# A fused attention, Fourier mixing and MLP kernel on one core: the written order of its work is replaced behind the last loads of the second weight matrix

## The chip, the cores and the metric

The kernel runs on one core of one Trainium2 chip. The metric is the time of one execution in microseconds of device time; less is better. A core has a matrix engine (TensorE, PE in the profile), a vector engine (VectorE, DVE), a scalar engine (ScalarE, ACT), a general engine (GpSimd, POOL) and a queue that only issues transfers (SyncE, SP). Each runs its own list of instructions strictly in order. What one needs of another, it waits for by semaphore, and everything behind a waiting instruction on that engine waits too. The matrix engine writes to banks of PSUM; an evacuation (an instruction of VectorE or ScalarE that reads a bank and writes to SBUF) makes a bank free again.

## The reference

```python
def attention(q, k, v, n_global, n_local):        # 4 batches, 8 heads, 768 rows, 64 wide
    scores = q @ k^T / 8 + bias                   # bias: -slope(head) * distance
    scores = where(is_global | is_local, scores, -1e9)  # 8 global keys, 96 local keys back
    a = exp(scores - max); a = a / sum(a)
    return a @ v
def moe(x, w1, w2):                               # x: attention out as (4, 768, 512); w1 512x2048, w2 2048x512
    mixed = real(fft(fft(x, axis=1), axis=2))
    u = x + mixed
    un = (u - mean(u)) / sqrt(var(u) + 1e-6)      # over the 512 features
    return u + relu(un @ w1) @ w2                 # the second u is the sum, not its norm
```

## The kernel before

The four batches go through the same stages, and the stages of different batches overlap.

*Attention.* q and k are loaded (GpSimd's queue casts them to half precision), transposed, and multiplied to scores in PSUM; ScalarE takes the exponential (`er`, L763), VectorE multiplies it with a mask that holds the bias (`ex`, L778; the mask `mk` is made by ScalarE, L1657), and TensorE multiplies with v (`av`, L822). The first rows of v are copied into `vB` (L793, L795). VectorE divides by the sums (`x`, L832 and L834).

*Mixing.* The two Fourier transforms are matrix products with cosine tables on folded halves of x: VectorE makes the folds (`f1`, `f2`, `f3`, `z`, `w`), TensorE the products `y` (L1105) and `u` (L1192). The rows of x are needed in another arrangement to be added: x is written to DRAM (`xd`; ScalarE's queue, L874), and read back by SyncE (`xr`, L884) and by a gather on GpSimd's queue (`xg`, L887), which takes its indices from `back`, that SyncE loads (L1608). In batch 1 the write consists of two transfers of 384 KB.

*Chunks.* A batch has three pairs of row blocks, so there are 12 chunks c = 0 to 11. Chunk 3 is the first of batch 1, 6 the first of batch 2. For each chunk VectorE adds u = x + mixed (`u c`, L1232 for most, L1244 to L1251 for the middle one of a batch, c = 1, 4, 7, 10, which needs xg), the row is centred (`un`, two halves, L1269 on ScalarE or L1271 on VectorE), transposed (`unT`; by a transfer of SyncE's from chunk 3 on, L1292), squared on ScalarE (`ss`, L1278), and the reciprocal deviation is made by GpSimd (`rstd`, L1285 and L1286).

*MLP.* The first product of a chunk has eight units `ph(c,0)` to `ph(c,7)` of eight matmuls of 256 columns each (L1339); each fills one bank, and its evacuation with the relu is `h c j` on ScalarE (L1344) or VectorE (L1345). The second product of chunks 0 and 1 is plain (`pg(c,t,part)`, L1370, each part with a quarter of w2; its sum into u is `ob`, L1381). From chunk 2 on it is a scheme with seven half products in place of eight, in units `p1`, `p45`, `p6`, `p7` and `p32` (L1484), which needs sums of h (`s 1` to `s 4`, VectorE, L1448 to L1461) and sums of w2. Of the sums of w2 there are `w2a` (L1420) and two folds `w2t 0` and `w2t 1` (L1424 to L1426, three instructions each), which are made once, by VectorE; `p45(2)` is the first that needs both folds. The results are added to u by VectorE (`ra`, `rd`, `ob`, L1502) and stored.

*What sets the order.* Everything is recorded as named units with the engines that may do it, and then put on the engines in the order of a table, `Plan.ORDER`, which holds for each of PE, ACT, DVE, POOL and SP a list of names (A for attention units, M for mixing, H for `ph`, G for the second product, T for the rest; `H27.0` is the first other operation that H27 issues). A name under ACT rather than DVE puts the operation on ScalarE. `Plan.run` (L291) walks the lists and keeps a clock for each engine with estimated costs; those estimates serve to find a table and to decide in which order the lists are emitted, and they are no part of what runs on the chip. PSUM banks and buffers are taken in rings in the order of the lists, so a unit waits for the evacuation of an earlier one that had the same bank.

## Time and profile before

| | |
|---|---|
| three runs | 246.40 us median, 246.03 to 246.49 |
| the profiled execution | 245.87 us; span in the trace 244.1 us |
| TensorE | busy 232.0 us of 244.1 |
| VectorE | busy 193.4 us |
| ScalarE | busy 138.8 us |
| GpSimd | busy 114.8 us, transfers that it issues included |
| DMA | 32.85 MB, mean 135 GB/s |

The profile is one execution. The span is the time from the first to the last instruction in the trace; 1.77 us of the execution lie around it. Rows of the timeline read: start, duration, engine, line of the kernel, operation, result and source, number of instructions, and in brackets how long the engine had been idle before and what it then waited for. The ends of matmuls are modelled, so that a unit of eight matmuls of 256 columns is shown with 1.04 us though the next one begins after 0.87 us.

### The profile page before, as it was taken

The page shows a single profiled execution, that of the slowest core. Times are in us where ns is not written, and L with a number is a line of the kernel's source. Part 1 is how long each engine was busy: PE and PEld are TensorE (multiplying, and loading weights), DVE is VectorE, ACT ScalarE, POOL GpSimd, SP SyncE. Part 2 cuts the span into 40 slices and gives each one's busy share as a digit, 9 for nine tenths or more (in the row PEclk, how much of TensorE's full clock was granted, in tenths as well). Part 3 has the DMA queues.
Part 4 walks back from the last instruction along what each step waited for, and adds up shares of the span by engine and source line. Part 5 has one row for each costly group of instructions (what it writes and reads, how often), then busy time and mean ns, then how long its engine had stood idle before and what let it go on. Part 6 is the DMA issues. An engine that isn't in the chain of part 4 may idle for free.

```text
span 244.1 us, 7606 instructions
## 1 busy us (share of the span) xinstructions
PE 232.0 (95%) x3251; PEld 191.2 (78%) x3251; DVE 193.4 (79%) x420; ACT 138.8 (57%) x226; POOL 114.8 (47%) x164
## 2 busy tenths in 40 slices
PE   7679899999999999999999999999999999999993
PEld 2557776878677667788989888898889898888883
DVE  2559997879972789999999889889998755846483
ACT  2368788864657468658357788364534651434200
POOL 8998898866590038999059056500300320011020
PEclk9997999999999999999999999999999999999999
DMA  6999999999999999999999979220570330040212
GB/s 170 181 169 145 157 235 172 197 190 196 110 145 152 234 179 205 117 135 110 242 184 285 135 84 156 46 33 13 174 258 4 77 99 0 1 130 1 89 72 99
DMA packets 95938, 32.85 MB, mean 135 GB/s; under 512 B 84160, under 2 KB 92480, under 8 KB 95904
## 3 DMA queue, kind: packets, MB, share of 16 engines
q0 software_dynamic: 66176, 17.06, 71.7%
q1 hardware_dynamic: 26560, 12.56, 25.1%
q10 hardware_dynamic: 3168, 2.75, 4.1%
q8 instruction: 25, 0.41, 0.7%
q14 instruction: 9, 0.07, 0.1%
HBM read 31.44 MB, written 8.65 MB: 164 GB/s over the span
## 4 chain that ended last, share of the span: by engine, by line
PE 67%; DMA 14%; DVE 5%; ACT 5%; POOL 3%; issue 3%; SPq 1%; POOLq 0%
PE ph L1339 29%; PE pgD L1484 14%; PE pgA L1484 10%; DMA qk<-in_q_dram 4%; DMA v<-in_v_dram 4%; PE py L1105 3%; DMA hT<-in_q_dram 3%; PE pg L1370 3%; PE pav L822 3%; ACT ex L766 2%; DMA back<-backm 2%; DMA xr<-xd,back 2%; PE sc L737 2%; PE pu L1192 1%; ACT mk L1657 1%
## 5 line engine op out<-in xcount | busy, mean ns | idle before, releaser
L1339 PE MATMUL ph<-unT,w 128*128 128x256 f16 x768 | 94.4, 273 | 0.8 <-issue 0.4
L1339 PEld LDWEIGHTS <-w 128*128 128x128 f16 x768 | 73.6, 98 | 12.5 <-issue 1.2
L1344 ACT ACTIVATE hT<-ph 128x512 f16<-128x512 f32 x73 | 42.9, 596 | 54.6 <-PE ph L1339 52.6
L1484 PEld LDWEIGHTS <-hT 128*128 128x128 f16 x320 | 31.0, 98 | 4.3 <-issue 0.4
L1285 POOL TENSOR_SCALAR sm<-sm 128x2 f32<-128x2 f32 x12 | 3.4, 284 | 58.2 <-ACT un L1278 57.8
L763 ACT ACTIVATE er<-sc 128x1024 f16<-128x1024 f32 (+1 forms) x24 | 22.3, 951 | 11.4 <-PE sc L737 8.2
L1345 DVE TENSOR_SCALAR hT<-ph 128x512 f16<-128x512 f32 x23 | 15.7, 687 | 12.7 <-PE ph L1339 12.7
L766 ACT ACTIVATE ex<-sc 128x1024 f16<-128x1024 f32 (+1 forms) x24 | 21.7, 955 | 7.1 <-PE sc L743 6.9
L1502 DVE SCALAR_TENSOR_TENSOR u<-pgA,sm,u 128x256 f32<-128x256 f32 (+1 forms) x30 | 16.9, 568 | 6.4 <-PE pgA L1484 6.0
L1502 DVE SCALAR_TENSOR_TENSOR u<-pgD,sm,u 128x512 f32<-128x512 f32 (+1 forms) x21 | 15.2, 722 | 3.5 <-PE pgD L1484 3.3
L1355 POOL DMA_INDIRECT out_dram<-u,back x4 | 4.5, 1120 | 27.5 <-DVE rev L1140 16.3
L887 POOL DMA_INDIRECT xr<-xd,back x3 | 4.8, 1602 | 25.4 <-PE pg L1370 16.1
L1370 PE MATMUL pg<-w,hT 128*128 128x512 f16 x64 | 16.0, 379 | 0.0
L1118 ACT ACTIVATE zy<-py 128x1024 f16<-128x1024 f32 (+1 forms) x13 | 11.1, 857 | 8.4 <-PE py L1105 6.1
L778 DVE TENSOR_TENSOR ex<-er,mk 128x1024 f16<-128x1024 f16 (+1 forms) x24 | 15.1, 646 | 0.7 <-ACT er L763 0.7
L1278 ACT ACTIVATE un<-un 128x512 f16<-128x512 f16 x24 | 15.0, 625 | 1.1 <-DMA unT<-un 1.1
L552 POOL DMA_DIRECT2D qk<-in_k_dram x16 | 13.7, 903 | 1.2 <-DMA w<-in_moe_w_ch_dram 0.8
L1269 ACT ACTIVATE un<-u,sm 128x512 f16<-128x512 f32 x19 | 13.1, 717 | 1.9 <-DVE sm L1251 0.7
L552 POOL DMA_DIRECT2D qk<-in_q_dram x16 | 13.6, 870 | 0.0
L822 PEld LDWEIGHTS <-ex 128*128 128x128 f16 x352 | 12.4, 97 | 1.1 <-ACT ex L766 0.4
L834 DVE TENSOR_TENSOR x<-pav,rc 128x384 f16<-128x384 f32 x24 | 12.6, 554 | 0.6
L822 PE MATMUL pav<-v,ex 128*128 128x65 f16 x224 | 12.9, 193 | 0.2
(170 smaller groups left out, 492.9 us busy)
## 6 DMA issues: line engine op xcount, KB each, us to landing
w<-in_moe_w_ch_dram POOLq DMA_DIRECT2D x8, 512.0 KB, 13.4
out_dram<-u SPq DMA_DIRECT2D x15, 256.0 KB, 3.0
v<-in_v_dram POOLq DMA_DIRECT2D x12, 192.0 KB, 5.8
qk<-in_k_dram POOLq DMA_DIRECT2D x16, 96.0 KB, 5.4
qk<-in_q_dram POOLq DMA_DIRECT2D x16, 96.0 KB, 4.5
xr<-xd SPq DMA_DIRECT2D x3, 512.0 KB, 4.6
xd<-x ACTq DMA_DIRECT2D x2, 768.0 KB, 4.5
v<-in_v_dram POOLq DMA_DIRECT2D x8, 96.0 KB, 7.0
```

The costliest lines, as they stand in the source:

```text
L552: nc.gpsimd.dma_start(qk16[n][:, w, :, h], src[b, h0 + h].rearrange("(i m) d -> m i d", m=P))
L763: A(mine(), cut(pa), AF.Exp, 0.0, 0.125)
L766: A(cut(expst[hp][:, :, g * 512:g * 512 + (384 if g == 2 else 512)]), cut(pa), AF.Exp, 0.0, 0.125)
L778: VT(o, mine(), m, op=ALU.mult)
L822: nc.tensor.matmul(o[:, s * 65:(s + 1) * 65], lhsT, w, start=(a == 0), stop=(a == len(ops) - 1), skip_group_check=True)
L1278: A(x, x, AF.Square, accum_out=MV[c][:, a, 2:3])
L1339: nc.tensor.matmul(ph[:, a * CH:(a + 1) * CH].rearrange("p (x m) -> p x m", x=2), W1[0][:, d, jb * P:(jb + 1) * P], UNT[c][:, :, d, :], st ...
L1344: pl.later([("ACT", act(512), lambda: A(dst, ph, AF.Relu)), ("DVE", dve(512), lambda: V.tensor_scalar_max(dst, ph, 0.0))], [], e, [("h", c ...
L1345: ("DVE", dve(512), lambda: V.tensor_scalar_max(dst, ph, 0.0))],
L1370: nc.tensor.matmul(pg, HT[c][:, jb, t * P:(t + 1) * P], W2[0][:, jb, :], start=(jb == 0), stop=(jb == NJ - 1))
L1484: nc.tensor.matmul(o, lhs(j), rhs(j), start=(first and j == 0), stop=(j == NK - 1), skip_group_check=True)
L1502: V.scalar_tensor_tensor(o, x, r(t), acc, op0=ALU.mult, op1=ALU.add)
```

## The change

The table keeps its order in the first 57 us of the run: TensorE's list is the same up to `ph(1,4)`, and those of the other engines up to about there. Behind that all five lists are new. TensorE has the same 3251 matmuls in another sequence. Among other things:

- GpSimd issues all loads of q, k and v of batch 2 first; `rstd 1` stood in the midst of them and now stands behind.
- Operations change their engine: two copies of `vB` go from GpSimd to ScalarE, one more `vB` and the mirrored rows `r` of batches 1 and 2 (three copies each, L1139 to L1141) from GpSimd to VectorE, one `vB` from VectorE to GpSimd; 19 operations from VectorE to ScalarE (16 evacuations `h`, one small scaling in chunk 2, a half `un` of chunks 3 and 4), 16 from ScalarE to VectorE (13 `h`, one `y` evacuation of batch 1, a half `un` of chunks 3 and 11).
- The last instruction of six `u` evacuations, 128x2 elements, multiplies with a tile and a constant instead of a constant.
- The estimates in `Plan` are changed. A way to make the sums `s` on GpSimd is added and the table doesn't use it.

The diff, of which the table's new rows are left out but for two:

```diff
@@ class Plan @@
+    ALONE = 1.54
-    LAT = {"ACT": 0.14, "DVE": 0.12, "POOL": 0.08}
+    LAT = {"ACT": 0.18, "DVE": 0.12, "POOL": 0.08}
...
     ORDER = {
         "PE": (
...
-            "A39 A29 M3 M9 A32 M7 A33 A40 M8 M10 A31 M6 A27 M11 M13 A44 H2 H7 A43 H4 H3 M12 A42 H0 H1 A41 H12 G4 H13 H11 G0 H6 H5 M14 G1 G5 G6 H15 G7 H14 "
+            "A39 A29 M3 M9 A32 M7 A33 A40 M8 M10 A31 M6 A27 M11 M13 A44 H2 H7 A43 H4 H3 M12 A42 H0 H1 A41 H12 H6 G4 G0 H13 G5 G1 H5 M14 H10 G6 G2 G3 H8 "
...
+        def cp_act():
+            A(vB[hp], v16[b % 2][:, h, 1:NS - 1, :], AF.Copy)
+            for r in rows:
+                A(vB[hp][r], head(r), AF.Copy)
-        pl.later([("POOL", 0.6 + 0.6 * len(rows), lambda: cp(nc.gpsimd)), ("DVE", 0.3 + 0.3 * len(rows), lambda: cp(V))], after, 0.0, [("vB", b, hp)], rank=RA(b))
+        pl.later([("POOL", 0.6 + 0.6 * len(rows), lambda: cp(nc.gpsimd)), ("DVE", 0.3 + 0.3 * len(rows), lambda: cp(V)), ("ACT", act(528) * (1 + len(rows)), cp_act)], after, 0.0, [("vB", b, hp)], rank=RA(b))
...
-            V.tensor_scalar_mul(sm[:, :, 1], sm[:, :, 0], -SC / Dm)
+            V.scalar_tensor_tensor(sm[:, :, 1], sm[:, :, 0], 2 * SC / Dm, mhalf, op0=ALU.mult, op1=ALU.mult)
...
+        def slow(fn):
+            return [("POOL", pool2(NK * P), lambda: fn(nc.gpsimd))] if c > 2 else []
...
-        pl.later([("DVE", us, s1)], hs + sfree(0), 0.0, [("s", c, 1)], rank=1)
+        pl.later([("DVE", us, s1)] + slow(s1), hs + sfree(0), 0.0, [("s", c, 1)], rank=1)
```

The lists of a few places follow, as they stand on the engines; the number behind a tile's name tells tiles of one kind apart.

**First place: the way of batch 1's x.** GpSimd before, in the loads of q and k of batch 2 (`qk`); `sm_1` is the tile that `rstd 1` works on:

```order
L552 DMA qk_4_1504<-in_k_dram 128x6x64
L552 DMA qk_2_1488<-in_k_dram 128x6x64
L552 DMA qk_5_1124<-in_k_dram 128x6x64
L1285 TENSOR_SCALAR sm_1_1013<-sm_1_1013 128x2
L1286 TENSOR_TENSOR sm_1_1013<-sm_1_1013,mhalf_78 128x2
L552 DMA qk_2_1488<-in_k_dram 128x6x64
L552 DMA qk_4_1504<-in_k_dram 128x6x64
L552 DMA qk_3_1036<-in_k_dram 128x6x64
```

GpSimd after, from the same load on:

```order
L562 DMA qk_4_1504<-in_k_dram 128x6x64
L562 DMA qk_2_1488<-in_k_dram 128x6x64
L562 DMA qk_5_1124<-in_k_dram 128x6x64
L562 DMA qk_4_1504<-in_k_dram 128x6x64
L562 DMA qk_3_1036<-in_q_dram 128x6x64 x2
L562 DMA qk_4_1504<-in_q_dram 128x6x64 x2
L562 DMA qk_3_1036<-in_k_dram 128x6x64
L562 DMA qk_2_1488<-in_q_dram 128x6x64
L532 DMA v160_84<-in_v_dram 128x12x64
L562 DMA qk_2_1488<-in_k_dram 128x6x64
L1299 TENSOR_SCALAR sm_1_1013<-sm_1_1013 128x2
L1300 TENSOR_TENSOR sm_1_1013<-sm_1_1013,mhalf_78 128x2
```

The loads of q, k and v stand together, and `rstd 1` behind the last of them. ScalarE before, where it issues the two writes of x to `xd` (L874); `zy` is the evacuation of `y`, `mk` the mask, `hT` an evacuation `h`:

```order
L1344 ACTIVATE hT_3_1538<-ph_1_0_1744 128x512
L1657 ACTIVATE mk_76<-distk_74 128x640
L874 DMA xd_1_1780<-tt_1_1401 64x6x512
L1118 ACTIVATE zy_3_1753<-py_1_1_1782 128x1024
L874 DMA xd_1_1780<-tt_1_1401 64x6x512
L1657 ACTIVATE mk_76<-distk_74 128x640 x4
L1344 ACTIVATE hT_4_1792<-ph_2_4_1813 128x512
```

ScalarE after:

```order
L1292 ACTIVATE un_2_1530,sm_2_1250<-un_2_1530 128x512
L1292 ACTIVATE un_1_1332,sm_1_1013<-un_1_1332 128x512
L1674 ACTIVATE mk_76<-distk_74 128x640 x2
L1358 ACTIVATE hT_4_1752<-ph_2_1_1753 128x512
L888 DMA xd_1_1780<-tt_1_1411 64x6x512 x2
L1674 ACTIVATE mk_76<-distk_74 128x640 x3
L1292 ACTIVATE un_2_1530,sm_2_1250<-un_2_1530 128x512
L1674 ACTIVATE mk_76<-distk_74 128x640
```

The two writes are one behind the other, and the evacuation of `py_1_1` that stood between them is no longer there (VectorE has it).

**Second place: the second fold of w2.** VectorE before, from the end of `u 4` on; the three rows with `w2_0` and `tt` are `w2t 1`, `eg_91` is `s 1` of chunk 2:

```order
L1249 TENSOR_TENSOR sm_4_2075<-sm_4_2075 128x2
L1250 TENSOR_TENSOR sm_4_2075<-sm_4_2075,u_6_2074 128x2
L1251 TENSOR_SCALAR sm_4_2075<-sm_4_2075 128x2
L1424 TENSOR_TENSOR w2_0_711<-w2_0_711 128x4x256
L1425 TENSOR_TENSOR tt_2_1996<-w2_0_711 128x1024
L1426 TENSOR_TENSOR tt_2_1996<-w2_0_711,tt_2_1996 128x1024
L778 TENSOR_TENSOR ex2_82<-er_4_2030,mk_76 128x2x384
L1448 TENSOR_TENSOR eg_91<-hT_4_1792 128x1024
L778 TENSOR_TENSOR ex0_80<-er_5_2085,mk_76 128x2x512
```

VectorE after, from the end of `u 4` on:

```order
L1265 SCALAR_TENSOR_TENSOR sm_4_2068<-sm_4_2068,mhalf_78 128x2
L788 TENSOR_TENSOR ex0_80<-er_4_2020,mk_76 128x2x512
L1153 COPY rev0_1_2124<-zy_3_1733 128x2
L1154 COPY rev0_1_2124<-zy_3_1733 128x2x127
L1155 COPY rev0_1_2124<-zy_3_1733 128x256
L788 TENSOR_TENSOR ex2_82<-er_5_2065,mk_76 128x2x384
L1285 TENSOR_SCALAR un_4_2168<-u_6_2067,sm_4_2068 128x512
L1438 TENSOR_TENSOR w2_0_713<-w2_0_713 128x4x256
L1439 TENSOR_TENSOR tt_2_2008<-w2_0_713 128x1024
L1440 TENSOR_TENSOR tt_2_2008<-w2_0_713,tt_2_2008 128x1024
L1462 TENSOR_TENSOR eg_91<-hT_4_1752 128x1024
```

Two products `ex`, the three copies of mirrored rows (`rev0`) and a half `un 4` now stand ahead of the fold.

**Third place: the end.** VectorE before, from the last chunk's `s 1` on (`pgA_11`, `pgD_11` and `pgA_10`, `pgD_10` are banks of the last two chunks; L1448, L1454, L1461, L1451 are `s 1`, `s 2`, `s 4`, `s 3`):

```order
L1448 TENSOR_TENSOR mk_76<-hT_13_4340 128x1024
L1502 SCALAR_TENSOR_TENSOR u_12_3931<-pgA_10_4388,sm_10_3932,u_12_3931 128x256
L1454 TENSOR_TENSOR mk_76<-mk_76,hT_13_4340 128x1024
L1502 SCALAR_TENSOR_TENSOR u_12_3931<-pgD_10_4421,sm_10_3932,u_12_3931 128x512
L1502 SCALAR_TENSOR_TENSOR u_12_3931<-pgA_10_4388,sm_10_3932,u_12_3931 128x512
L1461 TENSOR_TENSOR mk_76<-hT_13_4340,mk_76 128x1024
L1451 TENSOR_TENSOR hT_13_4340<-hT_13_4340 128x8x128
L1502 SCALAR_TENSOR_TENSOR u_13_4090<-pgA_11_4497,sm_11_4091,u_13_4090 128x256
L1502 SCALAR_TENSOR_TENSOR u_13_4090<-pgD_11_4508,sm_11_4091,u_13_4090 128x512
L1502 SCALAR_TENSOR_TENSOR u_13_4090<-pgA_11_4497,sm_11_4091,u_13_4090 128x256
```

VectorE after:

```order
L1359 TENSOR_SCALAR hT_13_4339<-ph_11_4_4467 128x512
L1462 TENSOR_TENSOR mk_76<-hT_13_4339 128x1024
L1519 SCALAR_TENSOR_TENSOR u_12_3957<-pgD_10_4386,sm_10_3958,u_12_3957 128x512
L1468 TENSOR_TENSOR mk_76<-mk_76,hT_13_4339 128x1024
L1519 SCALAR_TENSOR_TENSOR u_13_4199<-pgA_11_4495,sm_11_4200,u_13_4199 128x256
L1475 TENSOR_TENSOR mk_76<-hT_13_4339,mk_76 128x1024
L1465 TENSOR_TENSOR hT_13_4339<-hT_13_4339 128x8x128
L1519 SCALAR_TENSOR_TENSOR u_13_4199<-pgD_11_4506,sm_11_4200,u_13_4199 128x512
L1519 SCALAR_TENSOR_TENSOR u_13_4199<-pgA_11_4495,sm_11_4200,u_13_4199 128x256
```

An evacuation of the last chunk stands directly ahead of its sums, one sum of chunk 10 (`pgA_10`) is ahead of them, and `s 4` and `s 3` stand behind the first `pgA_11`.

91 lines of the change are left out of this document (49 added, 42 removed), and 52 rows, old and new, of the table ORDER.

## The prediction

> **What bounds the kernel now.** I read first the busy times of the engines, then busy time by stretch, then what TensorE waits for. In the stretches the columns are start:end, length, and busy us with number of instructions for PE, PEld, DVE, ACT and POOL, then granted clock, DMA share and GB/s.
>
> ```profile
> PE 232.0 (95%) x3251; PEld 191.2 (78%) x3251; DVE 193.4 (79%) x420; ACT 138.8 (57%) x226; POOL 114.8 (47%) x164
> ```
>
> ```profile
> 57.40:82.40 25.00, 25.00 (x218) 17.65 (x214) 18.37 (x35) 14.70 (x28) 10.56 (x14) 1.00 1.60 161
> 82.40:112.10 29.70, 28.75 (x477) 22.25 (x474) 27.27 (x63) 20.00 (x33) 21.87 (x27) 1.00 1.42 159
> 112.10:240.40 128.30, 128.30 (x1494) 113.74 (x1484) 104.25 (x215) 64.56 (x113) 32.22 (x43) 1.00 0.55 104
> ```
>
> TensorE is the bound. It is busy throughout the first and the third stretch, at full granted clock; only 82 to 112 us hold idle time, 29.70 - 28.75 = 0.95 us. All its waits behind 57.4 us, where the change begins, are three lines, and two of the idle spells look as follows:
>
> ```profile
> PE ph L1339 <- DMA unT<-un: 0.4, 1, 0.4
> PE pgA L1484 <- DVE u L1502: 0.3, 1, 0.3
> PE sc L737 <- ACT er L763: 0.2, 1, 0.2
> ```
>
> ```profile
> 94.34 1.14 PE L1339 MATMUL ph<-unT,w 128*128 128x256 f16 x9 [0.37 <-DMA unT<-un]
> ...
> 104.90 1.03 PE L1484 MATMUL pgA<-misc,hT 128*128 128x256 f16 x8 [0.31 <-DVE u L1502]
> ...
> 109.73 1.04 PE L1484 MATMUL pgD<-w,sb 128*128 128x256 f16 x8
> 110.61 1.04 PE L1484 MATMUL pgD<-w,hT 128*128 128x256 f16 x8
> ```
>
> The last two rows are an undisturbed pair: the second unit begins 0.16 us before the first one's modelled end (109.73 + 1.04 = 110.77). A start behind an idle spell loses that overlap too. So the four spells (there are two smaller ones at 100.9 and 103.5) cost 0.95 us plus up to 4 x 0.16 = 0.6: 1.5 us is all that a new order with the same matmuls can win, and every new wait in the 154 us without any is a loss. That asymmetry is the base of what follows.
>
> The chain that ended last shows where the 0.95 us are from (the "issue" and short rows are left out):
>
> ```profile
> 83.26 4.77 DMA back<-backm
> ...
> 88.94 3.98 DMA xr<-xd,back
> ...
> 92.95 0.87 DVE u L1244 x2
> ...
> 104.90 1.03 PE pgA L1484 x8
> ```
>
> x of batch 1 goes to DRAM and back late, u 3 and u 4 start late on VectorE, and VectorE then stays behind TensorE up to 105 us.
>
> **The change, step 1: loads, writes and reads of batch 1's x earlier.**
>
> ```profile
> 75.54 1.04 PE L1339 MATMUL ph<-unT,w 128*128 128x256 f16 x8
> 84.86 1.06 PE L1192 MATMUL pu<-t,zy 128*128 128x128 f16 x16
> ```
>
> ```profile
> 63.80 0.26 POOL L1285 TENSOR_SCALAR sm<-sm 128x2 f32<-128x2 f32 x1 [4.75 <-ACT un L1278]
> 64.15 1.03 POOL L1286 TENSOR_TENSOR sm<-sm,mhalf 128x2 f32<-128x2 f32 x1
> 65.14 2.56 POOL L552 DMA_DIRECT2D qk<-in_k_dram  x3
> ...
> 71.09 1.72 POOL L552 DMA_DIRECT2D qk<-in_q_dram  x2
> ```
>
> ```profile
> 73.12 0.66 ACTq L874 DMA_DIRECT2D xd<-tt  x1
> ...
> 75.74 0.58 ACTq L874 DMA_DIRECT2D xd<-tt  x1
> ```
>
> ```profile
> DMA to landing us min/median/max: 6.3/6.7/7.2
> ```
>
> ```profile
> DMA to landing us min/median/max: 3.7/3.7/3.7
> ```
>
> GpSimd stands 4.75 us for the squares on ScalarE (the row calls them un) and 1.3 us in `rstd 1` with nine loads behind it; they are issued from 65.14 to 72.81. Without it they can start at 59.05, six us earlier; since earlier loads have to land before, I take four. The two writes of x (first landing figure) then meet fewer loads. They took 6.3 and 7.2 us and landed at 80.30 and 75.74 + 6.3 = 82.02; batch 3's write, alone, took 3.7 (second figure). After the change both are issued together, when ScalarE comes to `h 2 1`. ph(2,1) began at 75.54; the new list has two `ph` units (0.87 each) and a `y` (0.95) less ahead of it and step 2's 0.3 us more, so it ends near 74.1, and the writes are issued at about 74.2. With a landing time between 3.7 and 7.2 that is 77.9 to 81.4; I take 80.0, nearer to the slow end, as the transposes of batch 2 still run beside them. Against 82.02 that is 2.0 us earlier (0.6 to 4.1).
>
> ```profile
> 82.21 0.52 SPq L884 DMA_DIRECT2D xr<-xd  x1
> ```
>
> ```profile
> 87.17 0.69 DVE L1232 SCALAR_TENSOR_TENSOR u<-pu,xr 128x512 f32<-128x512 f32 x1 [0.83 <-PE sc L737]
> ...
> 91.19 0.69 DVE L778 TENSOR_TENSOR ex<-er,mk 128x1024 f16<-128x1024 f16 x1
> 91.79 0.74 DVE L1381 SCALAR_TENSOR_TENSOR u<-pg,sm,u 128x512 f32<-128x512 f32 x1
> 92.95 0.87 DVE L1244 SCALAR_TENSOR_TENSOR u<-pu,xr 128x384 f32<-128x384 f32 x1 [0.41 <-DMA xr<-xd,back]
> ...
> 95.55 0.68 DVE L1424 TENSOR_TENSOR w<-w 128x1024 f16<-128x1024 f16 x1
> ...
> 97.07 0.77 DVE L1426 TENSOR_TENSOR tt<-w,tt 128x1024 f16<-128x1024 f16 x1
> ...
> 100.57 0.73 DVE L1271 TENSOR_SCALAR un<-u,sm 128x512 f16<-128x512 f32 x1
> ```
>
> The read xr follows 0.2 us behind the write and u 3 came 4.96 us after it (the row names TensorE, which had long been done). Now u 3 can start at 82.02 + 0.19 + 4.96 - 2.0 = 85.2; the product u(3) itself, one part pg (0.87) earlier and 0.3 later than its row, ends at 85.3 and VectorE wakes at about 85.5, so 85.5 is taken, 1.7 us earlier. The indices `back`, whose load SyncE issues at 83.26 behind a store, now come directly behind xr, so the gather is earlier by as much, and u 4's wait of 0.41 us goes as well. The first idle spell (unT 3) goes. VectorE keeps the same sum of work up to the sums of batch 2: less the wait of 0.41 and one half `un` (0.65 from 100.57 to the next), plus one more `ob` (0.66) and the mirrored rows (0.42 on VectorE). So it is 1.7 us ahead and the spells behind it go: of 1.5 us I take 1.2, since the new list puts scores in pairs behind each other again, and their banks wait for ScalarE as at 100.9. Bounds: 0 to -1.5.
>
> Within this step the second fold of w2 has three us more ahead of it: two `ex` (0.6 each), mirrored rows 0.42, half an un 0.65, an `ob` 0.66. By these durations it ends 13.0 to 13.4 us behind the start of u 3, before 10.6 (97.07 + 0.7 - 87.17). TensorE wants it for p45(2), 6.6 us behind the start of ph(3,0) (five `ph` and p1 at 0.87 each and four scores at 0.35). ph(3,0) without its wait is due at 94.34 - 0.37 - 0.87 (p1 no longer ahead) + 0.3 = 93.4, so p45(2) at 100.0. With u 3 at 85.5 the slack is over 1 us; at 87 it is nil.
>
> **Step 2: an early use of w2.** The second quarter's load ends here, and it was first used at 64.02:
>
> ```profile
> 47.59 0.74 POOL L1679 DMA_DIRECT2D w<-in_moe_w_ch_dram  x1
> ```
>
> ```profile
> DMA to landing us min/median/max: 14.4/14.4/14.4
> ```
>
> It lands at 62.0. In the new list pg(0,t1,1) stands behind ph(1,4), ph(0,6), two parts pg and ph(1,5), five units of 0.87 from 57.45 on: due at 61.8. A wait of 0.3 us with the wake-up (0 to 0.5).
>
> **Step 3: batch 2's stretch, 112 to 160 us.** Two groups give the durations (busy us, mean ns of one, idle before):
>
> ```profile
> L834 DVE TENSOR_TENSOR x<-pav,rc 128x384 f16<-128x384 f32 x24 | 12.6, 554 | 0.6
> L1269 ACT ACTIVATE un<-u,sm 128x512 f16<-128x512 f32 x19 | 13.1, 717 | 1.9 <-DVE sm L1251 0.7
> ```
>
> p45(3) takes the bank that `ob 2 1` frees, which now stands behind an `x` item (two of 0.55 and a reciprocal); by the list it comes 0.2 us late. ph(6,1) needs the bank of an `h` on ScalarE which now has half an un (0.72) and a square ahead: 0.25 late. I found the other late transfers of the new lists (unT 5, 9, 11 and the reads of batches 2 and 3) with slacks between 0.4 and 3 us, and cost them at nothing; what covers them is TensorE's queue of `ph` units, and if one is later than that, it costs its lateness one to one. Bounds of the step: 0, as TensorE had no wait here, to 1.5, if three such slacks of half a us are gone.
>
> **Step 4: the end.**
>
> ```profile
> 236.82 0.75 DVE L1502 SCALAR_TENSOR_TENSOR u<-pgD,sm,u 128x512 f32<-128x512 f32 x1 [0.40 <-PE pgD L1484]
> ```
>
> This frees the bank for the last but two product 2.7 us behind the start of p45(11) at 234.87. In the new list the evacuation of ph(11,4) (0.69), `s 1`, a sum of chunk 10, `s 2`, the first `pgA_11`, `s 4` and `s 3` stand ahead of it in one string, and only two products lie between ph(11,4) and p45(11): it ends 2.96 us behind. +0.25 (0 to 0.6).
>
> Small edits together: the `vB` copies on ScalarE cost about 0.6 each like its evacuations of 512 columns and lie beside TensorE, as ScalarE is idle 9.7 of 29.7 us; the 128x2 instruction has the same size in its new form. Both 0; for all six of the latter at most 6 x 0.2 us on VectorE.
>
> **The sum**: -1.2 + 0.3 + 0.2 + 0.25 + 0.25 = -0.2 us. The profiled execution took 245.87 (span 244.1 and 1.77 around it), 0.53 below the median, so against the median: 246.4 - 0.2 = 246.2 us.
>
> A rule stands against step 1. The trace first: the nine loads cost GpSimd 0.85 us each (2.56 us for three) while VectorE ran folds like the row below, and landed within 3.0 to 6.1 us.
>
> ```profile
> 65.72 0.95 DVE L1061 TENSOR_TENSOR eA<-zy 128x1536 f16<-128x1536 f16 x1
> ```
>
> ```profile
> DMA to landing us min/median/max: 3.0/4.0/6.1
> ```
>
> The Trainium skill, "SBUF — State Buffer", section "SBUF: two separate sides", says that VectorE and GpSimd share a port pair as an exclusive lock, and that a transfer issued by GpSimd starves while VectorE runs two-port operations, since GpSimd can't write the descriptors. By that rule the loads, now beside the folds of batch 1, would gain nothing; this trace doesn't agree so far, since loads went out beside such a fold.
>
> **The rivals.** *A, the forecast*: x is back 1.7 us earlier and the later places take back most of it: 246.2.
>
> *B, slower: ScalarE and VectorE stand in their queues.* `un 3 1` is now on ScalarE, ahead of `h 2 0` and everything behind it. And ph(3,0) started 94.34 - 87.17 = 7.2 us behind u 3, through unT 3, while it is now due at 93.4. So if u 3 starts later than about 86.2, which is so if the writes land behind 81.0, TensorE waits, first for the `h` that stand behind `un 3 1`, then for unT 3. With u 3 where it was, ph(3,0) starts at 94.34 as before, but p1(2) (0.87) is still to be done behind it. Of the 1.5 us only the spells behind it can go, some 0.6. With steps 3 and 4 that is 246.4 + 0.87 - 0.6 + 0.7 = 247.4, and 247.9 if p45(2) waits 0.5 for the fold. For it: the writes are close together and DMA is busy at the same share (1.60 and 1.42). Against: four us fewer loads.
>
> *C, the starved loads*: the loads beside the folds are not earlier, nor the writes: u 3 stays at 87.2, and the time is B's, 247.4.
>
> *D: x is earlier, but the slacks of step 3 don't hold*; three or four new waits of 0.3 to 0.5 between 112 and 240 us, beyond the sum: 246.2 + 1.2 = 247.4. For it: 128 us without a wait have no way to get better.
>
> *E: nothing measurable*: new waits equal those removed, 246.4; it lies within A.
>
> **How the numbers follow.** A 0.52, B 0.24, C 0.06, D 0.18. 0.2% or 0.5 us is about what a measurement can tell from no change here: faster is below 245.9, slower above 246.9. A's own range is 245.2 (no wait in steps 2 to 4: 246.4 - 1.2) to 247.0 (its steps at their upper bounds in part): 0.30 faster, 0.20 same, 0.02 slower. B, C and D give 0.06 same and 0.42 slower. So 0.30, 0.26, 0.44; the forecast stays the likeliest case's, 246.2. The range of 8 in 10 goes from 245.1 to 248.2: B at its worst and D with one wait more.
>
> **What would show it.** Step 1: no rstd among the qk loads, writes landed near 80, u 3 near 85.5, no wait for unT at ph(3,0). Step 2: a wait of about 0.3 of pg for the w load near 62. Step 3: TensorE waits of 0.2 at p45(3) and ph(6,1). Step 4: the last matmul 0.25 later behind p45(11). B: u 3 behind 86.2, and waits of ph(2,6), ph(2,7) or p45(2). D: several waits for `hT` or `u` behind 112 us. The forecast is wrong above all if the xd writes land where they did, or if TensorE's new waits behind 112 us sum to over 1 us.

## The result, and the profile after

| | before | changed |
|---|---|---|
| median of 20 runs | 247.2 us (245.68 to 249.2) | 249.5 us (247.56 to 252.16) |
| ratio | 1 | 1.0064, 95% interval 1.0036 to 1.0092 |
| the profiled execution | 245.87 us, span 244.1 | 249.77 us, span 247.9 |

The changed kernel is 0.64% slower, some 1.6 us (0.9 to 2.3), where 0.2 us faster was forecast. The median of three that the forecast stood on, 246.4, was a low draw of a kernel whose executions spread over 3.5 us; the ratio is what counts. It leaves out three slow executions of the changed kernel, more than 1.5% above its fastest, so it is smaller than the quotient of the two medians, 1.0093.

The page's first line of the changed kernel, its busy time by stretch (columns as in the prediction), and all that TensorE waits for behind 57.4 us:

```profile
PE 231.1 (93%) x3251; PEld 190.5 (77%) x3251; DVE 194.0 (78%) x423; ACT 140.5 (57%) x233; POOL 105.0 (42%) x154
```

```profile
57.40:82.40 25.00, 23.91 (x215) 16.43 (x213) 18.68 (x36) 13.02 (x27) 11.05 (x15) 1.00 1.68 155
82.40:112.10 29.70, 28.69 (x447) 22.81 (x447) 24.98 (x59) 22.40 (x36) 18.98 (x24) 1.00 1.51 162
112.10:244.20 132.10, 130.92 (x1537) 115.28 (x1534) 108.26 (x225) 66.64 (x120) 25.79 (x36) 1.00 0.59 101
```

```profile
PE ph L1353 <- ACT hT L1358: 1.1, 1, 1.1
PE pg L1384 <- DMA w<-in_moe_w_ch_dram: 1.0, 1, 1.0
PE pgA L1501 <- DVE u L1519: 0.5, 1, 0.5
PE pgD L1501 <- DVE u L1519: 0.2, 1, 0.2
```

GpSimd has 10 us less, TensorE is still the bound at full clock. The three waits that the prediction counted on (unT 3, an exponential, `ra 2 1`) are all gone. Four others stand in their place, and two of the stretches that had none have over 1 us each.

A profile shows one execution, and the front of the run, whose order is the same in all kernels here, is not the same length twice. Two lines of TensorE's waits up to 57.4 us, of the kernel before and of the changed one, and the same instruction's line in e10, below:

```profile
PE py L1105 <- issue: 0.6, 1, 0.6
```

```profile
PE py L1119 <- issue: 1.8, 1, 1.8
```

```profile
PE py L1115 <- issue: 3.0, 1, 3.0
```

In 17 profiles ph(1,4), the last unit ahead of the new order, starts between 56.84 and 60.87 us. So I compare from there on, by the starts of six units that all orders share. The table, in us, has the time from each to the next; the columns are named by where they end.

| kernel | ph(1,4) at | ph(4,0) | u(6) | y(b3,0) | p45(11) | last product | end of span |
|---|---|---|---|---|---|---|---|
| before | 57.45 | 54.68 | 21.88 | 45.67 | 55.19 | 4.49 | 4.72 |
| before, second profile (c2) | 59.02 | 56.15 | 21.88 | 45.67 | 55.19 | 4.49 | 4.73 |
| changed | 58.57 | 55.61 | 21.88 | 46.97 | 55.19 | 4.60 | 5.08 |
| changed, second profile (c1) | 58.79 | 55.59 | 21.88 | 46.90 | 55.19 | 4.60 | 5.07 |
| e1 | 58.60 | 54.09 | 21.91 | 46.26 | 55.19 | 4.60 | 5.09 |
| e2 | 60.83 | 53.65 | 22.03 | 47.99 | 55.19 | 4.60 | 5.09 |
| e3 | 58.10 | 54.76 | 22.00 | 47.56 | 55.19 | 4.60 | 5.08 |
| e4 | 60.81 | 54.04 | 21.91 | 46.39 | 55.19 | 4.60 | 5.08 |
| e5 | 57.40 | 54.66 | 23.75 | 45.91 | 55.19 | 4.60 | 4.76 |
| e6 | 59.86 | 64.34 | 21.88 | 45.91 | 55.19 | 4.60 | 5.08 |
| e7 | 58.32 | 54.31 | 21.88 | 45.66 | 55.19 | 4.49 | 4.72 |
| e8 | 56.84 | 53.65 | 21.88 | 45.66 | 55.19 | 4.49 | 4.72 |
| e9 | 59.03 | 54.06 | 21.88 | 46.79 | 55.19 | 4.60 | 5.09 |
| e10 | 60.87 | 53.73 | 21.88 | 46.90 | 55.19 | 4.60 | 5.08 |
| e11 | 59.66 | 55.04 | 21.88 | 46.63 | 55.19 | 4.60 | 5.21 |
| e12 | 58.84 | 53.24 | 21.88 | 47.94 | 55.19 | 4.60 | 5.08 |
| e13 | 57.25 | 54.65 | 22.07 | 47.32 | 55.19 | 4.60 | 5.09 |

Between the two profiles each of the kernels as they are, the mean differences are +0.2 us up to ph(4,0), +1.3 between u(6) and y(b3,0) and +0.5 behind p45(11) (0.11 and 0.35): 1.9 us, which lies in the interval of the measured 1.6. The first of these is the least sure: the two profiles of before differ by 1.5 us there, and e1 and e5, which have the changed kernel's order up to ph(4,0), took 54.09 and 54.66, so that the mean of four is 0.4 below before's. The other two come out the same in both profiles. From y(b3,0) to p45(11), 55 us, the new order changes nothing.

**Where the waits are from.** The first is the w2 load. GpSimd's issue, and TensorE's use:

```profile
49.57 0.74 POOL L1696 DMA_DIRECT2D w<-in_moe_w_ch_dram  x1
```

```profile
64.06 1.89 PE L1384 MATMUL pg<-w,hT 128*128 128x512 f16 x8 [0.97 <-DMA w<-in_moe_w_ch_dram]
```

It was issued 2 us later than in the profile of before, took 14.4 us again, and landed at 64.0. The second is on ScalarE (the ACTq row is the issue of both writes of x):

```profile
76.33 3.27 ACTq L888 DMA_DIRECT2D xd<-tt  x2
79.65 1.99 ACT L1674 ACTIVATE mk<-distk 128x640 f16<-128x640 f16 x3 [2.75 <-issue]
...
82.78 0.57 ACT L1358 ACTIVATE hT<-ph 128x512 f16<-128x512 f32 x1
```

```profile
83.41 1.03 PE L1353 MATMUL ph<-unT,w 128*128 128x256 f16 x8 [1.12 <-ACT hT L1358]
```

The first write's issue took 0.65 us and the second's 2.6; ScalarE stood idle for 2.75 us, `h 1 6` came late, and ph(2,2) waited for its bank. The third and fourth are on VectorE, at u 7 (L1258), with `ra 4 1` (144.46) behind it:

```profile
140.93 0.86 DVE L1258 SCALAR_TENSOR_TENSOR u<-pu,xr 128x384 f32<-128x384 f32 x1 [2.26 <-DMA out_dram<-u]
...
144.46 0.47 DVE L1519 SCALAR_TENSOR_TENSOR u<-pgA,sm,u 128x256 f32<-128x256 f32 x1
```

```profile
144.99 1.03 PE L1501 MATMUL pgA<-misc,hT 128*128 128x256 f16 x8 [0.48 <-DVE u L1519]
...
147.18 1.03 PE L1501 MATMUL pgD<-w,sb 128*128 128x256 f16 x8 [0.24 <-DVE u L1519]
```

u 7 writes to a buffer that the store of `ob 3 0` has to read first. From issue to landing that store took, in the changed kernel and before:

```profile
DMA to landing us min/median/max: 7.8/7.8/7.8
```

```profile
DMA to landing us min/median/max: 4.7/4.7/4.7
```

Before, u 7 waited for it too (0.4 us), but `ra 4 1` stood ahead of u 7.

### The profile page after: what moved, and what is told of

Its sections match the earlier page's. It is cut to its first block, busy times and chain, and to the rows that moved or that the text cites. A ratio compares the mean times of both kernels' runs of the same rounds, so it can differ in the third digit from the quotient of the medians.

```text
span 247.9 us, 7610 instructions
## 1 busy us (share of the span) xinstructions
PE 231.1 (93%) x3251; PEld 190.5 (77%) x3251; DVE 194.0 (78%) x423; ACT 140.5 (57%) x233; POOL 105.0 (42%) x154
## 3 DMA queue, kind: packets, MB, share of 16 engines
q10 hardware_dynamic: 3168, 2.75, 3.6%
## 4 chain that ended last, share of the span: by engine, by line
PE 57%; DMA 17%; DVE 11%; POOL 6%; ACT 4%; issue 2%; ACTq 1%; DVEq 0%; POOLq 0%
PE ph L1353 25%; PE pgD L1501 11%; PE pgA L1501 8%; DMA w<-in_moe_w_ch_dram 6%; DMA v<-in_v_dram 5%; PE pg L1384 4%; DMA hT<-in_q_dram 3%; DMA out_dram<-u 3%; DVE u L1519 3%; PE sc L747 2%; PE pav L836 2%; ACT ex L776 2%; PE pu L1206 2%; PE py L1119 2%; ACTq L888 1%
## 5 line engine op out<-in xcount | busy, mean ns | idle before, releaser
L1358 ACT ACTIVATE hT<-ph 128x512 f16<-128x512 f32 x76 | 44.8, 595 | 53.6 <-PE ph L1353 53.4
L1299 POOL TENSOR_SCALAR sm<-sm 128x2 f32<-128x2 f32 x12 | 2.9, 244 | 78.6 <-ACT un L1292 78.5
L1359 DVE TENSOR_SCALAR hT<-ph 128x512 f16<-128x512 f32 x20 | 13.6, 686 | 5.3 <-PE ph L1353 5.2
L1369 POOL DMA_INDIRECT out_dram<-u,back x4 | 5.2, 1301 | 26.9 <-DVE u L1519 22.1
L1384 PE MATMUL pg<-w,hT 128*128 128x512 f16 x64 | 15.3, 379 | 1.0 <-DMA w<-in_moe_w_ch_dram 1.0
L1132 ACT ACTIVATE zy<-py 128x1024 f16<-128x1024 f32 (+1 forms) x12 | 10.1, 845 | 5.8 <-DVE eA L1089 2.5
L1119 PE MATMUL py<-t,ww 128*128 128x256 f16 x80 | 11.4, 273 | 0.6 <-ACT ex L776 0.6
```

The lines of the kernel that those rows point to most:

```text
L1119: nc.tensor.matmul(o, lhsT, rhs, start=(x == 0), stop=(x == len(ops) - 1))
L1358: pl.later([("ACT", act(512), lambda: A(dst, ph, AF.Relu)), ("DVE", dve(512), lambda: V.tensor_scalar_max(dst, ph, 0.0))], [], e, [("h", c ...
L1384: nc.tensor.matmul(pg, HT[c][:, jb, t * P:(t + 1) * P], W2[0][:, jb, :], start=(jb == 0), stop=(jb == NJ - 1))
```

## The experiments

All edits are of the order table; in the diffs below only the moved names and their neighbours stand. Ratios are to the kernel before, with their 95% intervals.

**Theory W and rival F.** W: the loss is the sum of these waits. F: it lies in the front of the run, which was 1.1 us later in the changed kernel's profile.

**e1**, u 7 (`M23.6`) behind `s 4 3` (`T.216`) and `ra 4 1` (`G28.0`):

```diff
         "DVE": (
-            ... M23.0 M23.6 T.216 G28.0 A63.1 ...
+            ... M23.0 T.216 G28.0 M23.6 A63.1 ...
```

> The changed kernel, with u 7 on VectorE behind s 4 3 and ra 4 1 instead of ahead of them (ra 4 1 stood ahead of u 7 before the change too). Theory W (the loss is a sum of new waits at three places): u 7 still stands about 2 us for its buffer, which a store frees, but ra 4 1 no longer behind it; TensorE's waits at p7(4) (0.5) and p32(4) (0.2) go, the time falls by 0.7 to 1.1 us against the changed kernel. Rival F (the loss lies in the front of the run, which has the same order in both and was 1.1 us late in the changed kernel's profile): the waits may go, but the time stays where the changed kernel's is, at 1.006 of before.

1.0031 (0.9998 to 1.0065): half the loss seems gone, but the interval overlaps the changed kernel's. The profile says more. VectorE's and TensorE's waits, of the stretch from 130 to 146 us and of all behind 57.4:

```profile
DVE u L1515 <- PE pgA L1497: 0.9, 1, 0.9
DVE u L1254 <- DMA out_dram<-u: 0.4, 1, 0.4
```

```profile
PE sc L743 <- DMA qkT<-qk: 0.5, 1, 0.5
```

VectorE now waits for TensorE ahead of `ra 4 1`, as it did before the change, and TensorE's two waits for `ra 4 1` are gone. That holds throughout: all five profiles with u 7 ahead of `ra 4 1` in the new order (the changed kernel's two, e2, e3, e12) have these waits, and none of the eight with e1's edit has. u(6) to y(b3,0) falls from 46.9 to 46.3, not to 45.67: u 7 still comes late, and it also holds a bank that a score unit needs (the qkT wait above is elsewhere, at 87.6 us). In this profile the waits at w2 and at ph(2,2) aren't there either, with the same order at those places: they aren't in every execution.

**e2**, three mask instructions between the two writes of x (`T.89`, `T.90`):

```diff
         "ACT": (
-            ... T.89 T.90 T.44 T.40 T.47 M13.6 ...
+            ... T.89 T.44 T.40 T.47 T.90 M13.6 ...
```

> The changed kernel, with three mask instructions of ScalarE (0.73 us each) between the two writes of x to xd, which the changed kernel issues back to back. Theory W: the second issue took 2.6 us and kept ScalarE idle since the first still filled the queue; apart it takes 0.6 to 0.8, h 1 6 is 1.5 us or more earlier and TensorE's 1.1 us wait at ph(2,2) is gone; time 0.5 to 1.1 us less, if u 3 isn't later for it. If the queue is full for another reason (the transposes of batch 2 on SyncE), the issue takes as long apart and the wait stays. Rival F: no change of the time.

1.0081 (1.0041 to 1.012): no gain that the time shows, though its profile has no wait at ph(2,2) and 53.65 us up to ph(4,0). What happens is best seen in e10, which has this edit too, on ScalarE:

```profile
77.49 0.67 ACTq L884 DMA_DIRECT2D xd<-tt  x1
...
78.29 2.65 ACTq L884 DMA_DIRECT2D xd<-tt  x1
78.85 1.35 ACT L1670 ACTIVATE mk<-distk 128x640 f16<-128x640 f16 x2
80.99 0.63 ACT L1288 ACTIVATE un<-un 128x512 f16<-128x512 f16 x1 [0.79 <-issue]
```

The second issue takes as long, so it isn't slow for being back to back. But the mask instructions were handed to ScalarE ahead of it and run meanwhile: 0.79 us idle in place of 2.75, and ph(2,2) doesn't wait. In the profiles with the changed kernel's pair of writes or this edit the second issue took 2.5 to 2.8 us in about half, and 0.6 to 0.7 in the others; with the kernel before's distance of 2.6 us, 0.6 in all four. In the changed kernel's profile SyncE's issues of the same microseconds were slow too, 3.0 us for a transpose and 2.3 for a store. What decides was not found.

**e3**, ph(0,5) (`H5`) and the transposes of chunk 2 (`M14`) ahead of pg(0,t1,1) (`G5`):

```diff
         "PE": (
-            ... H13 G5 G1 H5 M14 H10 ...
+            ... H13 H5 M14 G5 G1 H10 ...
```

> The changed kernel, with ph(0,5) and the transposes of chunk 2 on TensorE ahead of the first use of the second quarter of w2 (1.3 us of other work). Theory W: the 1.0 us wait for that load at pg(0,t1,1) goes to 0 to 0.2 and the time falls by 0.3 to 0.8 us, since the lateness of the front moves the load's issue as well and part of it is not a wait in other executions. Rival F: no change of the time beyond 0.3 us.

1.0091 (1.0056 to 1.0127). The wait for w2 is gone, and one of 0.7 us for an evacuation `h` on ScalarE stands at the next unit. A wait traded for another; no gain.

**e4**, the three together:

> The three edits together. Theory W: the sum, 1.5 to 2.8 us less than the changed kernel, so 0.995 to 1.000 of before. Rival F: still 1.004 to 1.008 of before.

1.0026 (1.0 to 1.0052): its interval lies below the changed kernel's 1.0064, which speaks against F, but overlaps that kernel's own, and it is no better than e1. Nor does the table exclude F. The four profiles of the old order reach ph(1,4) at 57.9 us in the mean and the 13 of the new one at 59.1, with spreads of 2.2 and 3.6 us. The order up to there is the same, so nothing here says why they should differ, but that a part of the loss lies in the front is neither shown nor excluded.

**c1**, the changed kernel again:

> The changed kernel once more, unchanged, for a second profile. If the waits at w2 (1.0) and at ph(2,2) (1.1) belong to the order, they are here again; if they came from that one execution (the second write's issue took 2.6 us there, 0.65 in e1 and e3), they aren't, and from ph(1,4) to ph(4,0) it takes 53.6 to 54.3 us. The wait of u 7 for its buffer, about 2 us, is here again, and from u(6) to y(b3,0) it takes 46.9 us or more.

A time of 249.88; all four waits again (0.7 at w2, 1.3 at ph(2,2), 0.5 and 0.2 behind u 7's 2.1). So the first profile was no exception.

**e5**, the transposes `xb 14` (`T.182`, `T.183`) ahead of the stores, on top of e1:

```diff
         "SP": (
-            ... T.102 T.205 T.177 T.34 T.206 T.212 T.182 T.140 T.186 T.211 T.183 ...
+            ... T.102 T.205 T.177 T.182 T.183 T.34 T.206 T.212 T.140 T.186 T.211 ...
```

> As e1, and both transposes of batch 3's pair 2 (xb 14) on SyncE directly behind xb 12 1, ahead of store ob 2 0, as far forward as they stood before the change. Theory S (what makes u 7 late is the landing of store ob 3 0, 7.9 to 8.3 us after its issue against 4.7 before, since transposes and loads of batch 3 now move in the same microseconds): the store lands within 6 us, u 7's wait is under 0.2, and the part from u(6) to y(b3,0) falls from 46.26 us to 45.7, as before the change; time another 0.3 to 0.6 us below e1. Rival: the landing is slow because of GpSimd's loads of q, k and v (one took 12 us), then it stays at 7 us or more and nothing is won; with xb 12 and 14 in a row the store of ob 2 and the read xr 2 come later, and could cost up to 0.5 us.

u 7, the row of L1254 below, doesn't wait for the store any more, and u(6) to y(b3,0) takes 45.91, nearly the 45.67 of before.

```profile
139.93 0.48 DVE L1515 SCALAR_TENSOR_TENSOR u<-pgA,sm,u 128x256 f32<-128x256 f32 x1 [0.92 <-PE pgA L1497]
140.33 0.85 DVE L1254 SCALAR_TENSOR_TENSOR u<-pu,xr 128x384 f32<-128x384 f32 x1
```

That looks like theory S, that the transposes make the store slow. The store's own rows say otherwise. It is issued here, and in e1, with u 7's row in e1 below it:

```profile
131.48 0.55 SPq L1616 DMA_DIRECT2D out_dram<-u  x1
```

```profile
131.53 0.34 SPq L1616 DMA_DIRECT2D out_dram<-u  x1
139.56 0.87 DVE L1254 SCALAR_TENSOR_TENSOR u<-pu,xr 128x384 f32<-128x384 f32 x1 [0.35 <-DMA out_dram<-u]
```

In e1 u 7 could start 8.0 us behind the store's issue; in e5 it came 8.85 us behind it, so it would not have had to wait for a store as slow as e1's. And the store was as slow: its last packet in the trace ends 7.8 us behind the issue, against 7.4 in e1, 7.2 in the changed kernel and 4.2 before. What spared u 7 the wait is that TensorE came to u(6) later, 4.3 us behind the store's issue in place of 3.1, since it had to stand for the table `c t1` (`T.34`), which the edit moves back by 3 us. e6, below, has e1's edit without this one, no wait of u 7, and 45.91 too. So the place of xb 14 is not what makes the store slow, and what does stays open. The rival named in the expectation, GpSimd's loads, was not tested.

The time is 1.0079 (1.0042 to 1.0117). The wait for `c t1` costs more than was won (23.75 us from ph(4,0) to u(6) in place of 21.9); the second line is another wait, at 82 us, far ahead of the edited place:

```profile
PE py L1115 <- DMA t<-t1m: 1.7, 1, 1.7
PE sc L743 <- DMA qkT<-qk: 1.1, 1, 1.1
```

**e6**, `rstd 1` back in the midst of the loads, on top of e1, and **e7**, the kernel before with `rstd 1` (`M8.8`) behind them:

The diff is e7's; e6 goes the other way in the changed kernel's list.

```diff
         "POOL": (
-            ... T.120 M8.8 T.106 T.116 ... T.113 T.109 T.92 ...
+            ... T.120 T.106 T.116 ... T.113 T.109 M8.8 T.92 ...
```

> As e1, and rstd 1 on GpSimd back in the midst of the loads of batch 2, behind the load of qk 11 1 0, as before the change. Theory L (the stretch up to ph(4,0) is 0.6 to 1.0 us shorter in the changed kernel because x of batch 1 is back earlier, and that because the loads are earlier): GpSimd stands again at rstd 1, now until the squares behind ph(1,0), some 10 us; loads, transposes and the write of x are later, u 3 starts 1.5 us or more later counted from ph(1,4), and from ph(1,4) to ph(4,0) it takes 55 us or more in place of 54.1. Rival O (the stretch is shorter by the new order of TensorE and VectorE alone): still 53.7 to 54.3 us.

> The kernel before, with one edit: rstd 1 on GpSimd behind the last load of batch 2, as the change has it. Theory L: the loads are issued 4 to 6 us earlier, x is back 0.5 to 2 us earlier, the waits of 0.95 us between 94 and 105 us shrink by half or go, from ph(1,4) to ph(4,0) 53.3 to 54.2 us in place of 54.7, time 0.3 to 1.2 us less than before. Rival O: no change within 0.3 us; rstd 1 late could also hold back the sums ob of chunk 1 and cost up to 0.5 us.

e6: 1.0509 (1.0447 to 1.0571). From ph(1,4) to ph(4,0) it takes 64.34 us; u 3 and all that follows is 10 us late, and TensorE stands at the scores of batch 2:

```profile
PE sc L743 <- DMA qkT<-qk: 8.1, 1, 8.1
```

The new order puts the squares for `rstd 1` so late that it needs the loads ahead. The edit is too strong to price the loads, and it doesn't decide between L and O either: loads ten us late would hold up any order. e7 comes nearer: 54.31 in place of 54.68 (or of 56.15, in c2 below), ph(3,0) no longer waits, and the time is 0.9991 (0.9956 to 1.0026), no change that can be told. Why it isn't more, GpSimd's rows in e7 show:

```profile
61.99 0.83 POOL L548 DMA_DIRECT2D qk<-in_k_dram  x1 [2.28 <-DMA w<-in_moe_w_ch_dram]
64.11 0.82 POOL L548 DMA_DIRECT2D qk<-in_k_dram  x1 [1.30 <-DMA w<-in_moe_w_ch_dram]
...
69.33 1.69 POOL L548 DMA_DIRECT2D qk<-in_q_dram  x2
```

With `rstd 1` out of the way GpSimd stands for the loads of w2 to land. The issue of the last load of q ends at 71.0 in place of 72.8: 1.8 us earlier (2.7 counted from ph(1,4)), not four.

**e8**, e7's edit and on VectorE `ra 2 1` (`G18.0`) ahead of two products `ex`:

```diff
         "DVE": (
-            ... T.204 A56.1 A50.1 G18.0 M17.7 ...
+            ... T.204 G18.0 A56.1 A50.1 M17.7 ...
```

> The kernel before with two edits: rstd 1 behind the loads of batch 2 (as in e7), and on VectorE ra 2 1 ahead of the two products ex that stood directly ahead of it. TensorE's wait of 0.3 us at p7(2) is for ra 2 1. If the waits of the kernel before are each worth what the trace shows: from ph(1,4) to ph(4,0) 53.8 to 54.0 us (54.68 before, 54.31 in e7), to the last product 181.0 to 181.2, time 0.996 to 0.998 of before. If the two ex then come late for the scores' banks, the wait only moves there and nothing is won over e7.

**0.9961 (0.9927 to 0.9996): faster than both kernels**, though against the one before the interval only just excludes no change. From ph(1,4) to ph(4,0) it takes 53.65 us, and TensorE has no wait left behind the front. The stretch that held 0.95 us of idle time:

```profile
82.40:112.10 29.70, 29.59 (x488) 23.33 (x487) 28.29 (x64) 21.71 (x34) 23.45 (x30) 1.00 1.42 152
```

In this profile the waits of before are gone, by two edits in place of five new lists.

**c2**, the kernel before again:

> The kernel before once more, for a second profile. If the front of the run (up to ph(1,4), the same order in both kernels) varies by itself, ph(1,4) starts anywhere from 57.4 to 60.8 us as it did with the other kernels (57.45 in the first profile of before), and from there to the last product it takes 181.7 to 182.2 us again. If the front of the kernel before is faster by itself, it starts at 57.4 to 57.7 again.

ph(1,4) starts at 59.02, so the front varies by itself. But so does the stretch that the prediction took its gain from: 56.15 us up to ph(4,0) in place of 54.68, and 183.4 to the last product, where 181.7 to 182.2 was expected. TensorE's waits in c2 sum to 2.4 us:

```profile
PE pgA L1480 <- DVE u L1498: 1.0, 1, 1.0
PE sc L733 <- ACT er L759: 0.6, 1, 0.6
PE pu L1188 <- ACT er L759: 0.5, 1, 0.5
PE ph L1335 <- DMA unT<-un: 0.3, 1, 0.3
```

**e9** (e1, e2, and on SyncE xr 2 (`T.140`), xb 14 0 and 14 1 ahead of xb 15 1, behind `c t1`) and **e10** (e1 and e2):

```diff
         "SP": (
-            ... T.34 T.206 T.212 T.182 T.140 T.186 T.211 T.183 ...
+            ... T.34 T.206 T.212 T.140 T.182 T.183 T.186 T.211 ...
```

> The changed kernel with e1's and e2's edits, and on SyncE the read xr 2, then xb 14 0 and xb 14 1, directly behind the table c t1 and the stores of ob 2 1 and 3 1. Theory S (the store of ob 3 0 lands late because xb 14 and 15 move at the same time): u 7 doesn't wait, from u(6) to y(b3,0) 45.7 to 45.9 us, and with e2's gain up to ph(4,0) (53.65 from ph(1,4)) 181.0 to 181.6 us from ph(1,4) to the last product, time 0.995 to 0.999 of before. If the store still takes over 7 us, 46.3 as in e1.

> The changed kernel with e1's and e2's edits alone. If both effects are what their profiles showed and add up: no wait at ph(2,2), 53.6 to 54.1 us from ph(1,4) to ph(4,0), 46.2 to 46.4 from u(6) to y(b3,0), 181.6 to 182.0 in all (181.92 before): time 0.997 to 1.002 of before. If the loss lies elsewhere: 1.003 or more.

e9 1.0039 (1.0001 to 1.0077), e10 1.0031 (0.9994 to 1.0067). Up to ph(4,0) e10 is where it was expected (53.73) and e9 0.4 us above (54.06); between u(6) and y(b3,0) both lose (46.79, 46.90), u 7 waiting 0.8 and 1.3 us for its store. In e9, with both transposes xb 14 ahead of it, the store's last packet still ends 7.5 us behind the issue: as in e5, their place doesn't make it fast.

**e11** (e1, and the two `vB` copies `T.124` and `T.172` from ScalarE back on GpSimd) and **e12** (the last w2 load, `T.63`, ahead of `vB 1 2`, `T.87`):

```diff
         "POOL": (
-            ... T.64 T.87 T.63 T.121 ...
+            ... T.64 T.63 T.87 T.121 ...
```

> As e1, and the two copies of vB that the change gives to ScalarE (batch 2 pair 1, batch 3 pair 0) back on GpSimd, as before the change. Two questions. First, what the copies on ScalarE are worth: they lie beside TensorE's work in the profiles, so from ph(1,4) to the last product 181.6 to 182.6 us as in e1, e4 and e10; if they delayed the exponentials, 0.3 us less or more. Second, the end: from p45(11) to the end of the span it took 9.66 us in the changed kernel and e1 and 9.23 before, of which 0.10 lies before the last product and 0.32 in the last two steps of GpSimd, which are the same instructions in both kernels. If that hangs on where GpSimd's program ends (its number of instructions), it changes here, to 9.3 to 9.4; if it hangs on the stores or their order, it stays at 9.6 to 9.7.

> The changed kernel, with the last load of w2 on GpSimd ahead of the three copies of vB 1 2 (2.0 us) that stood ahead of it in both kernels. If the load's issue sets its landing: issued 2 us earlier, landed 1 to 2 us earlier, TensorE's wait at pg(0,t1,1) (1.0 and 0.7 us in two profiles) is gone, from ph(1,4) to ph(2,1) 15.5 us in place of 16.6 and 16.3; if it also was this wait that brought the second write of xd together with the transposes, its issue takes 0.7 us again and from ph(1,4) to ph(4,0) it takes 53.7 to 54.3; time 0.4 to 1.5 us below the changed kernel. If the load lands when it did because the loads ahead of it in the queue set its time (they landed at 57.8 and 61.5), nothing changes.

e11: 1.0069 (1.0039 to 1.0099), 0.4% above e1. At the place where I put the copies GpSimd was late with one:

```profile
110.08 0.19 PE L832 MATMUL pav<-vB,ex 128*128 128x65 f16 x1 [1.26 <-POOL vB L801]
```

So this edit says nothing against the copies on ScalarE. From p45(11) to the end it took 9.81 us, neither of the two values expected; the part on the hardware comes back to that.

e12: 1.0033 (0.9999 to 1.0068). GpSimd's load and TensorE's use of it:

```profile
47.28 0.74 POOL L1692 DMA_DIRECT2D w<-in_moe_w_ch_dram  x1 [0.46 <-DMA w<-in_moe_w_ch_dram]
```

```profile
63.18 1.89 PE L1380 MATMUL pg<-w,hT 128*128 128x512 f16 x8
```

The load landed at 62.3 in place of 64.0, the wait is gone, the second write's issue took 0.67 us, and ph(4,0) comes 53.24 us behind ph(1,4), the best of all. u 7 then waited 3.0 us and gave back 2.3 (47.94 against 45.67).

**e13**, e12 and e1 together:

> The changed kernel with both edits, e12's (last w2 load ahead of the copies) and e1's (u 7 behind s 4 3 and ra 4 1). If the loss of the changed kernel is the sum of the wait at the w2 load with what follows from it, of u 7's wait, and of 0.4 us at the end, then no wait at pg(0,t1,1) and ph(2,2), none for ra 4 1, 181.0 to 181.8 us from ph(1,4) to the last product (181.9 and 183.4 in the two profiles of before, 184.2 and 184.3 in those of the changed kernel), and a time of 0.997 to 1.002 of before. If a part of the loss is still unnamed, 1.003 or more.

1.0012 (0.9973 to 1.0051): level with before. TensorE's waits behind 55 us in its profile:

```profile
PE sc L743 <- DVE u L1258: 1.4, 1, 1.4
PE ph L1349 <- ACT hT L1354: 1.1, 1, 1.1
```

There is no wait for w2, yet the second write's issue took 2.6 us again (54.65 up to ph(4,0)). So the w2 wait isn't its cause, as e12 alone would have let one think. And u 7, behind `ra 4 1` now, still holds up a score unit. That the named parts make up the loss fits the time, within its interval of 0.4%, but this profile doesn't show it: from ph(1,4) to the last product it has 183.8 us, where 181.0 to 181.8 was expected and the changed kernel took 184.2. The execution is short because its front was, with ph(1,4) at 57.25.

## Why the prediction was wrong, point by point

**What bounds the kernel** held: TensorE, at full clock, with 0.95 us of waits to win and 154 us in which there was only something to lose. That asymmetry was seen and then not given its weight. The 0.95 us were those of one execution; in c2 the same kernel has 2.4.

**Step 1, the size of the gain (-1.2).** The waits it named all went: from ph(3,0) to ph(4,0) the changed kernel takes 17.7 us as before (55.61 - 37.90 and 54.68 - 36.89), with p1(2), 0.87 us, added. But the mechanism was mis-sized. "I take four" us for the loads is 1.8 in e7 (2.7 counted from ph(1,4)), because GpSimd's next limit was the landing of w2. "80.0" for the writes' landing is 83.84 with the front 1.1 us late, 25.3 us behind ph(1,4); before it was 82.02, 24.6 behind. In the changed kernel's two profiles they weren't earlier at all, which the prediction had named as a sign of being wrong; in the profiles where the second issue took 0.6 to 0.7 us they landed 23.2 to 24.4 behind. u 3 was earlier by 1.5 us in e1 (86.79 - 58.60 against 87.17 - 57.45), for the most part since the read xr behind the writes took 3.7 us and not 4.8. In the changed kernel's own profile, where xr took 3.7 us as well, u 3 is 0.35 us later (88.64 - 58.57): there it waited for the product u(3) itself, which TensorE's waits at w2 and ph(2,2) had made late.

**What step 1 left out.** "Both are issued together" was costed at the landing alone. The issue holds ScalarE's queue, 2.6 us in about half the profiles, and costs TensorE 1.1 to 1.3 where nothing was handed to ScalarE ahead of it (the changed kernel twice, e13). What is queued behind an issue has to be asked as with any wait.

**Step 2 (+0.3)** was right in kind; the wait was 1.0 and 0.7 us in the changed kernel's profiles, and 0.1 or none in the seven others with its order there, since both ends of it, TensorE's front and the load, vary by 1 to 3 us. Steps 1 and 2 together were put at -0.9 us, and up to ph(4,0) the profiles give +0.2 (two of each kernel) or -0.4 (with e1 and e5), so how far their size was off stays open.

**Step 3 (+0.45) is the step that failed.** It was +1.3 us, from u(6) to y(b3,0), in both profiles of the changed kernel. Neither p45(3) nor ph(6,1) waits. "Cost them at nothing" was wrong for a transfer that wasn't on the list at all: the store of `ob 3 0`, which frees u 7's buffer. The trace of before had a row that gave it away, among VectorE's waits from 130 to 146 us:

```profile
DVE u L1244 <- DMA out_dram<-u: 0.4, 1, 0.4
```

In the new list u 7 stands ahead of `ra 4 1`, so that TensorE waits for `ra 4 1` as well, and the store takes 7.8 us to land and not 4.7. The first half is shown by e1 and the other profiles with its edit: with it the stretch takes 46.5 us in the mean (45.91 to 47.32), without it 47.5 (46.90 to 47.99). Why the store is slow in the new order is not known; it is not the place of the transposes xb 14.

**Step 4 (+0.25)**: `rd 11 0` ended 2.80 us behind p45(11)'s start (41.04 - 38.24), 2.70 before; the last product is 0.11 late, and another 0.35 lies behind it, which no row of before could show.

**The rivals.** D, slacks that don't hold, is what happened (its 247.4 is +1.0 us, where 1.6 was measured), given 0.18. B had the right engine, ScalarE standing in its queue, at another place and for another reason. C, the starved loads: the issues took 0.82 to 0.85 us each beside VectorE's work, as before; what held them was the landing of w2 and no lock that these rows show. That the folds beside them are of the two-port kind was assumed in the prediction and isn't shown, so these rows don't test the rule.

## What to carry to other kernels

When TensorE is busy 95% and waits for 1 us, a whole new order has little to win and a hundred places to lose; mend the two waits one by one, as e8 did. In a new order look at every instruction that waits for a buffer, stores among what frees it, and ask what stands behind it on its engine. When an edit removes a wait, look at both ends of it: in e5 not the store but TensorE had moved. Compare kernels of the same front from the place where they part: the total varied by 3.5 us between executions, the stretch from y(b3,0) to p45(11) by less than 0.01.
